# Value tiles of 128 rows at a shift of 15 that serve both the block sums and half of the local attention

## The chip, the cores and the metric

The kernel runs on one core of a Trainium2 chip. The metric is the device time of one execution in microseconds (us), from launch to the last result in memory. Times of a kernel are given as the median of several runs; one further execution is recorded by the hardware profiler, and its rows are what the text quotes. KB and MB in the profile's list of transfers are 1024 and 1024 x 1024 bytes; GB/s are in powers of ten.

## The reference

Attention and a mixture of experts in sequence. Attention: batch 4, 8 heads, 768 positions, head size 64, all in float32. Every query sees the keys less than 16 positions away and, beside them, one summary key for each of the 24 blocks of 32 keys.

```python
k_sum = k.reshape(B, H, nb, block, D).max(axis=3)      # block = 32, nb = 24
v_sum = v.reshape(B, H, nb, block, D).mean(axis=3)
scores_l = scale * np.matmul(q, k.transpose(0, 1, 3, 2))
mask_l = np.abs(pos[:, None] - pos[None, :]) < window  # window = 16
scores_s = scale * np.einsum('bhsd,bhnd->bhsn', q, k_sum) + np.log(block)
scores_all = np.concatenate([np.where(mask_l, scores_l, -1e9), scores_s], axis=-1)
a = softmax(scores_all)
out = np.matmul(a, np.concatenate([v, v_sum], axis=2))
```

The 3072 output rows of 512 go to a noisy top-2 gate with 8 experts, each relu(x @ w1) @ w2 with an inner size of 1024, and the weighted results of the two experts are added.

## The kernel before

**Stages.** Attention takes about the first 145 us of the span, the experts the rest. Attention works on 24 tiles of 128 queries, six tiles to a batch; a tile consists of two blocks of 64 queries (blk 0 and 1). A block of queries needs the 94 keys and values that lie up to 15 positions around it, and the 24 block sums of its batch. The kernel lays both into one row of 118: the sums first (columns 0 to 23), then the 94 local ones. So every score matrix, every exp and every product with the values has 118 columns or rows.

**One step of the loop** (line 896, step t) does pieces of several tiles. TensorE: scores of tile t+2 (`scores`, L296, 32 matmuls of 64 queries by 118 keys, after `mask_sums`, L286, has written the mask of the next tile), transposes of the probabilities of tile t+1 (`p_trans`, L316), transposes of the result of tile t-1 for the gate (`x_pe`, L360), and the product with the values of tile t (`av`, L329). VectorE takes the row maxima (`smax`, L303) and divides (`norm`, L338 to L344). ScalarE does the exps (`sexp`, L310), copies the transposed probabilities (tile pts, L319), copies the transposed result (xt, L366) and makes its high half (xr, L349). GpSimd copies the keys of a tile into the joint row (kx, L114 and L120) and makes the low half of the result (L352). The gate's work for groups of four tiles is scattered between by hand, with `at(time, function)`, and so are the loads of later batches, the block sums and the first expert's weights.

**The values** are in DRAM with a column of ones behind each head (520 numbers a position) and 15 rows of zeros ahead. They are read twice. `load_vn` (L131) brings a batch into SBUF as six tiles of 128 positions (VN, in the memory that later holds the experts' hidden layer, hth). `v_sums` (L237) multiplies them with the 0/1 matrix ind of 24 columns and gets the block sums (48 matmuls, L241). `v_window` (L260) brings, for each block of 64 queries, a window of 96 positions into rows 24 to 119 of a buffer vw or htl; there are twelve such buffers, six for the batches of even and six for those of odd number. The sums are written to rows 0 to 23 of these buffers: for the first batch by VectorE, ScalarE and GpSimd to all six (L249, L250, L253), for a later batch by ScalarE to the first (L247) and by five DMAs of 24 rows to the other five (`v_rest`, L258).

**The order of the transfers** is that of SP's queue, which issues nearly all of them in program order. In step t that is: the query tile t+4 (`load_q`, L108), whatever `at` puts there (keys, L103; value tiles; copies of the sums; weights), the two windows of tile t+3 (`v_load`, after the av of tile t), and the result of tile t-2 (`x_out`, L355). The query tile that is issued in step t is used in step t+2. A window for tiles 3 to 5 of a batch waits until the av of three tiles before has read its buffer, and what stands behind it on SP waits too.

**At the end of attention** the rows of the first expert are gathered from the result in DRAM (xg <- xd, an indirect DMA of GpSimd), transposed by DMA, and the experts' matmuls begin (L727, L773).

Of the kernel before, what the change touches and what calls it, by code (L numbers as in the profile page):

```python
# [8 lines left out]
F32 = mybir.dt.float32  # L9
# [4 lines left out]
AF = mybir.ActivationFunctionType  # L14
# [3 lines left out]
B, H, S, D = 4, 8, 768, 64  # L18
BLK, WIN = 32, 16
NB = S // BLK  # L20
P = 128
TS = S // P
# [7 lines left out]
W = 64 + 2 * (WIN - 1)  # L30
NK = W + NB
PAD = WIN - 1
KW = S + 2 * PAD + 2
VR = 96
VP = S + VR - 64
H0 = 384
# [25 lines left out]
def attn_moe(ctx, tc, qt, kt, vt, wgn, noise, w1, w2, out):  # L62
# [31 lines left out]
    KB, VW, KX = [], [], []  # L94
# [15 lines left out]
    def kx_local(t):  # L110
        b, j = divmod(t, TS)
        k = KB[b % 2][:, :, j * P:j * P + 64 + W]
        for blk in range(2):
            (nc.vector if t < 2 else nc.gpsimd).tensor_copy(KX[t % QN][:, :, blk, NB:NK],  # L114
                                                            k[:, :, 64 * blk:64 * blk + W])

    def kx_sum(t):
        b, j = divmod(t, TS)
        if j < QN:
            (nc.gpsimd if b else nc.vector).tensor_copy(KX[t % QN][:, :, :, 0:NB],  # L120
                                                        KM[b][:, :, None, :].to_broadcast([P, HP, 2, NB]))
# [6 lines left out]
    VN = [flat[0][:, H * (D + 1) * j:H * (D + 1) * (j + 1)] for j in range(TS)]  # L128

    def load_vn(b, j):  # L130
        nc.sync.dma_start(VN[j].rearrange("p (h d) -> p h d", h=H), vt[b, PAD + j * P:PAD + (j + 1) * P])  # L131

# [30 lines left out]
    nc.vector.memset(masks[2][:, W - PAD:W], -1e9)  # L163

    ind = spare[0][:, :TS * NB].rearrange("p (t n) -> p t n", t=TS)
    nc.gpsimd.iota(ind, pattern=[[-P, TS], [BLK, NB]], base=0, channel_multiplier=-1,
# [3 lines left out]
    nc.vector.scalar_tensor_tensor(ind, ind, 0.0, ind0, op0=OP.is_le, op1=OP.mult)  # L170
    iota8 = const.tile([P, E], F32, name="iota8")
# [31 lines left out]
    for i in range(2):  # L203
        VW += [keep.tile([P, H, D + 1], F32, name=f"vw{4 * i + j}") for j in range(4)]
        VW += [flat[1][:, H * (D + 1) * j:H * (D + 1) * (j + 1)].rearrange("p (h d) -> p h d", h=H)
               for j in range(2 * i, 2 * i + 2)]
# [30 lines left out]
    def v_sums(b):  # L237
        pt = psum.tile([P, HP, P], F32, name="pt", bufs=2).rearrange("p a b -> p (a b)")
        for j in range(TS):
            for g in range(4):  # L240
                nc.tensor.matmul(pt[32 * g:32 * g + NB, 0:C4], ind[:, j, :], VN[j][:, C4 * g:C4 * g + C4],  # L241
                                 start=(j == 0), stop=(j == TS - 1), skip_group_check=True)
        x = [y[0:NB].rearrange("p h d -> p (h d)") for y in VW[(b % 2) * 6:(b % 2) * 6 + 6]]
        for g in range(4):
            i, o = pt[32 * g:32 * g + NB, 0:C4], slice(C4 * g, C4 * g + C4)
            if b:
                nc.scalar.activation(x[0][:, o], i, AF.Copy)  # L247
            else:
                nc.vector.tensor_copy(x[0][:, o], i)  # L249
                nc.scalar.activation(x[1][:, o], i, AF.Copy)  # L250
        if b == 0:
            for i in range(2, 6):
                nc.gpsimd.tensor_copy(x[i], x[i % 2])  # L253

    def v_rest(b):
        x = [y[0:NB] for y in VW[(b % 2) * 6:(b % 2) * 6 + 6]]
        for y in x[1:]:
            nc.sync.dma_start(y, x[0])  # L258

    def v_window(blk):  # L260
        b, j = divmod(blk, 2 * TS)
        x = VW[(b % 2) * 6 + j % 6]
        nc.sync.dma_start(x[NB:NB + VR], vt[b, 64 * j:64 * j + VR])
        return x
# [3 lines left out]
    def v_load(t):  # L268
        VX[t] = [v_window(2 * t), v_window(2 * t + 1)]
# [9 lines left out]
    def mask_sums(t):  # L279
        j = t % TS  # L280
        s = SC[t] = gate_space()[:, :, :SK].rearrange("p a (h k) -> p a h k", h=HP)
        for blk in range(2):
            for a in range(2):
                r = slice(64 * a, 64 * a + 64)
                m = masks[1 if (j, blk) == (0, 0) else 2 if (j, blk) == (TS - 1, 1) else 0]
                nc.tensor.matmul(s[64 * blk:64 * blk + 64, a, :, NB:], identb[r, r],  # L286
                                 m[r, None, :].to_broadcast([64, HP, W]), start=True, stop=False,
                                 skip_group_check=True)
# [509 lines left out]
    def at(t, f, *a):  # L798
        todo.setdefault(round(t, 3), []).append((f, a))
# [12 lines left out]
    for j in range(TS):  # L812
        load_vn(0, j)
# [11 lines left out]
    at(-0.9, v_sums, 0)  # L825

# [12 lines left out]
    for b in range(B - 1):  # L839
        for j in range(TS):  # L840
            at((6 * b + KP[j] if b else KP0[j]) + 0.1, k_piece, b + 1, j)
            if j % 3 == 0:
                at(6 * b + KL[j] if b else -1 + j // 3, load_k, b + 1, j, 3)
            at(VL[b][j], load_vn, b + 1, j)
        at(VS[b] + 0.2, v_sums, b + 1)
        at(VS[b] + 1.02, v_rest, b + 1)
# [298 lines left out]
def layout(q, k, v, moe_w_gate, moe_w_noise, moe_noise, moe_w1, moe_w2):  # L1145
# [9 lines left out]
    vp[:, PAD:PAD + S] = v1.transpose(0, 2, 1, 3)  # L1155
    wgn = np.zeros((P, DC, 4 * E), moe_w_gate.dtype)
# [23 lines left out]
```

## Time and profile before

| what | value |
|---|---|
| time, median of 3 runs | 698.92 us (696.99 to 701.62) |
| the profiled execution: its own time, its span | 698.5 us, 696.6 us |
| busy share of the span: PE, DVE, ACT, POOL | 94%, 46%, 34%, 36% |
| moved by DMA over the span | 125.88 MB, mean 181 GB/s |
| loads of value windows (32 to vw, 16 to htl) | 48 of 195 KB |
| loads of value tiles for the sums | 24 of 260 KB |

PE is TensorE, DVE VectorE, ACT ScalarE, POOL GpSimd, SP the engine that issues DMAs; SPq is its queue. An instruction is named by its line in the program, its engine, its operation, and what it writes and reads (out <- in), without buffer numbers. A bracket at the end of a row gives the time for which the engine stood idle ahead of it and what ended that. The chain of work that ended last is followed back from the last instruction to whatever released each step. PE's busy time is modelled, so a high share alone does not say that it is the bound; which wait ends last does.

### The profile page before, as it was taken

How to read it: one execution, taken by the hardware profiler on the slowest of the kernel's cores; microseconds unless marked ns; L12 is line 12 of the kernel's file. 1: busy time of each engine (PE TensorE's matmuls, PEld its weight loads, DVE VectorE, ACT ScalarE, POOL GpSimd, SP SyncE). 2: the span in 40 equal slices, each digit the busy share in tenths (PEclk: the TensorE clock that was granted, in tenths of full speed). 3: DMA queues.
4: the chain of work that ended last, by engine and by line, in shares of the span. 5: the costliest groups of instructions: out<-in, count | busy, mean ns of one | idle time of the engine just before them, and what ended most of it. 6: DMA issues, size and time to landing. Idle time of an engine off the chain costs nothing.

```text
span 696.6 us, 13835 instructions
## 1 busy us (share of the span) xinstructions
PE 654.1 (94%) x5408; PEld 378.9 (54%) x5408; DVE 317.1 (46%) x677; ACT 237.6 (34%) x543; POOL 253.9 (36%) x430
## 2 busy tenths in 40 slices
PE   7798999659899989999999999999999999999995
PEld 6676777535354644465446544654565456446542
DVE  5646788977863254226413521452154125312211
ACT  2887899744022143015202410340044015102200
POOL 3344366340531531553144323424350433222031
PEclk9999999989999999999999999999999999999999
DMA  9999897679555792559525951793199239421021
GB/s 278 316 256 319 273 317 230 200 141 403 139 174 117 187 320 77 171 181 283 189 94 132 219 191 71 176 253 133 63 247 220 94 109 272 109 79 60 1 88 47
DMA packets 101991, 125.88 MB, mean 181 GB/s; under 512 B 58621, under 2 KB 63493, under 8 KB 101916
## 3 DMA queue, kind: packets, MB, share of 16 engines
q1 hardware_dynamic: 90236, 88.64, 46.7%
q0 software_dynamic: 11680, 36.27, 17.4%
q8 instruction: 44, 0.72, 0.4%
q14 instruction: 31, 0.25, 0.1%
HBM read 86.82 MB, written 25.82 MB: 162 GB/s over the span
## 4 chain that ended last, share of the span: by engine, by line
PE 71%; issue 8%; DMA 7%; DVE 5%; POOL 4%; ACT 4%; SPq 1%; POOLq 0%; DVEq 0%; ACTq 0%
PE h L727 32%; PE pt L773 32%; DMA q<-in_qt_dram 3%; ACT p L310 2%; PE pt L769 2%; PE s L296 2%; DMA xg<-xd,tb 2%; PE o L329 1%; POOL kx L114 1%; POOL out_dram L87 1%; DMA kb<-in_kt_dram 1%; PE pt L316 1%; DVE w2l L665 1%; ACT pts L319 1%; DMA htl<-in_vt_dram 1%
## 5 line engine op out<-in xcount | busy, mean ns | idle before, releaser
L727 PE MATMUL h<-xte,w1h 128*128 128x384 f16 (+4 forms) x1024 | 197.3, 334 | 6.7 <-DMA xte<-xg 4.7
L731 ACT ACTIVATE hth<-h 128x384 f16<-128x384 f32 (+4 forms) x128 | 63.6, 500 | 317.5 <-PE h L727 309.7
L87 POOL DMA_INDIRECT out_dram<-y,tb x48 | 56.1, 1168 | 261.4 <-DVE y L782 231.4
L727 PEld LDWEIGHTS <-w1h 128*128 128x128 f16 x1024 | 100.3, 99 | 80.0 <-issue 10.0
L773 PEld LDWEIGHTS <-hth 128*128 128x128 f16 x768 | 75.1, 98 | 93.1 <-issue 3.9
L732 DVE SCALAR_TENSOR_TENSOR htl<-h,hth 128x384 f16<-128x384 f32 (+4 forms) x128 | 72.3, 569 | 102.4 <-ACT hth L731 91.2
L727 PE MATMUL h<-xte,w1l 128*128 128x384 f16 (+4 forms) x512 | 108.2, 334 | 0.0
L782 DVE SCALAR_TENSOR_TENSOR y<-pt,tb,prev 128x512 f32<-128x512 f32 x42 | 31.5, 751 | 168.0 <-PE pt L773 168.0
L773 PE MATMUL pt<-w2l,hth 128*128 128x512 f16 x384 | 91.2, 379 | 2.8 <-DVE w2l L665 2.8
L773 PE MATMUL pt<-w2h,hth 128*128 128x512 f16 x384 | 90.7, 379 | 0.0
L773 PE MATMUL pt<-w2h,htl 128*128 128x512 f16 x384 | 90.7, 379 | 0.0
L87 POOL DMA_INDIRECT xg<-xd,tb x53 | 59.5, 1123 | 70.5 <-DMA xte<-xg 41.6
L727 PEld LDWEIGHTS <-w1l 128*128 128x128 f16 x512 | 50.5, 99 | 36.7 <-issue 1.4
L773 PEld LDWEIGHTS <-htl 128*128 128x128 f16 x384 | 37.6, 98 | 45.0
L352 POOL TENSOR_TENSOR xr<-x,xr 128x512 f16<-128x512 f32 x24 | 28.2, 1174 | 69.4 <-ACT xr L349 61.2
L310 ACT ACTIVATE p<-s,nm 128x118 f32<-128x118 f32 x192 | 50.7, 376 | 0.8
L648 ACT ACTIVATE w2h<-stg 128x1024 f16<-128x1024 f32 x32 | 33.6, 1053 | 50.5 <-DMA stg<-in_w_dram 50.5
L665 DVE SCALAR_TENSOR_TENSOR w2l<-stg,w2h 128x1024 f16<-128x1024 f32 x32 | 38.8, 1221 | 23.2 <-ACT w2h L648 21.3
L87 POOL DMA_INDIRECT prev<-out_dram,tb x42 | 43.9, 1046 | 13.2 <-issue 13.2
L665 DVE SCALAR_TENSOR_TENSOR w1l<-stg,w1h 128x1024 f16<-128x1024 f32 x28 | 34.3, 1225 | 14.4 <-ACT w1h L648 13.6
L296 PE MATMUL s<-kx,q 64*64 64x118 f32 x768 | 28.4, 280 | 9.7 <-DMA q<-in_qt_dram 5.2
L316 PE MATMUL pt<-ident,p 128*118 128x128 f32 x192 | 29.3, 289 | 4.5 <-DVE lg L394 1.9
(173 smaller groups left out, 557.8 us busy)
## 6 DMA issues: line engine op xcount, KB each, us to landing
stg<-in_w_dram SPq DMA_DIRECT2D x64, 512.0 KB
hth<-in_vt_dram SPq DMA_DIRECT2D x24, 260.0 KB
vw<-in_vt_dram SPq DMA_DIRECT2D x32, 195.0 KB
q<-in_qt_dram SPq DMA_DIRECT2D x24, 256.0 KB
xd<-xr SPq DMA_DIRECT2D x24, 256.0 KB
out_dram<-xg SPq DMA_DIRECT2D x8, 768.0 KB
kb<-in_kt_dram SPq DMA_DIRECT2D x6, 768.0 KB
htl<-in_vt_dram SPq DMA_DIRECT2D x16, 195.0 KB
```

The source lines that it names most:

```text
L87: return nc.gpsimd.indirect_dma_start(**kw)
L296: nc.tensor.matmul(s[64 * blk:64 * blk + 64, a, hp, :], q[d, hp, blk], k[d, hp, blk, :], start=False, stop=hp == HP - 1, skip_group_check= ...
L310: nc.scalar.activation(PE_[t][:, a, hp, :], SC[t][:, a, hp, :], AF.Exp, bias=NM[t][:, 1, a, hp:hp + 1], scale=0.125)
L316: nc.tensor.transpose(pt[:NK, hp, :], PE_[t][:, a, hp, :], ident)
L352: nc.gpsimd.tensor_tensor(XR[t][:, DM:], X[t], XR[t][:, 0:DM], op=OP.subtract)
L648: nc.scalar.activation(WT[e][n + "h"][:, i % 4, :], SG[e, i], AF.Copy, scale=sc)
L665: nc.vector.scalar_tensor_tensor(lo, SG[e, i], sc, hi, op0=OP.mult, op1=OP.subtract)
L727: nc.tensor.matmul(ph[:, :n], w[wn][:, c, f * P:(f + 1) * P], x[:, xo + c, c0:c1], start=(k == 0), stop=(k == 11))
L731: nc.scalar.activation(hh[:, f, c0:c1], ph[:, :n], AF.Relu)
L732: nc.vector.scalar_tensor_tensor(hl[:, f, c0:c1], ph[:, :n], 0.0, hh[:, f, c0:c1], op0=OP.max, op1=OP.subtract)
L773: nc.tensor.matmul(py, hx[:, f, c * P:c * P + P], wv[:, f, :], start=(k == 0), stop=(k == 23))
L782: nc.vector.scalar_tensor_tensor(y, py[:, :d], gw, pv[:, :d], op0=OP.mult, op1=OP.add)
```

## The change

**One tile for two purposes.** The value tiles of 128 rows now begin 15 positions earlier: row r of tile j is position 128 j - 15 + r. Rows 0 to 95 are then the window of the tile's first block of 64 queries. The same tile serves the block sums, and once these are summed, they are written over its rows 96 to 119. So the first block's row of 120 is 96 local values and then 24 sums, and its keys are laid out in this order too (`L0[0] = 0`). The second block keeps a window of its own (VD), sums first, local values behind (`L0[1] = 24`). Both use 96 local keys instead of 94, with a mask that is two columns wider; NK goes from 118 to 120.

**The shift in the sums.** The six tiles of a batch cover positions -15 to 752. The last 15 positions are put in DRAM into the 15 rows ahead of the first, which were zeros; ind starts 15 later, and one column of it is set to 1 in rows 0 to 14 of the first tile. In the local attention of the batch's first block those rows are masked, as the zeros were.

**Buffers and transfers.** The value tiles have two buffers (VE, one in the memory of hth, one of its own), since they now live until the av of their tile. The windows are three for each parity of the batch (VD), one for a tile. The first batch's sums are copied by GpSimd to tiles 1 and 2 and to all windows, and by a DMA to tiles 3 to 5 (`v_rest(0)`, new in step 0). For a later batch one DMA writes five tiles and three write the windows. A tile's `v_load` issues one window.

```diff
-W = 64 + 2 * (WIN - 1)
+W = 64 + 2 * WIN
-    KB, VW, KX = [], [], []
+    KB, KX = [], []
+    L0 = (0, NB)
...
-            (nc.vector if t < 2 else nc.gpsimd).tensor_copy(KX[t % QN][:, :, blk, NB:NK],
+            (nc.vector if t < 2 else nc.gpsimd).tensor_copy(KX[t % QN][:, :, blk, L0[blk]:L0[blk] + W],
...
-    VN = [flat[0][:, H * (D + 1) * j:H * (D + 1) * (j + 1)] for j in range(TS)]
-
-    def load_vn(b, j):
-        nc.sync.dma_start(VN[j].rearrange("p (h d) -> p h d", h=H), vt[b, PAD + j * P:PAD + (j + 1) * P])
+    VE = [flat[0][:, :TS * VB].rearrange("p (j c) -> p j c", j=TS), keep.tile([P, TS, VB], F32, name="ve")]
+    VD = [[flat[1][:, VB * j:VB * (j + 1)] for j in range(3)],
+          [keep.tile([P, VB], F32, name=f"vd{j}") for j in range(2)] + [flat[1][:, 3 * VB:4 * VB]]]
+
+    def load_ve(b, j):
+        nc.sync.dma_start(VE[b % 2][:, j].rearrange("p (h d) -> p h d", h=H), vt[b, j * P:(j + 1) * P])
...
+    nc.vector.memset(ind[0:PAD, 0, NB - 1:NB], 1.0)
...
-        x = [y[0:NB].rearrange("p h d -> p (h d)") for y in VW[(b % 2) * 6:(b % 2) * 6 + 6]]
+        x, y = VE[b % 2][W:W + NB], [z[0:NB] for z in VD[b % 2]]
...
-                nc.scalar.activation(x[0][:, o], i, AF.Copy)
+                nc.scalar.activation(x[:, 0, o], i, AF.Copy)
             else:
-                nc.vector.tensor_copy(x[0][:, o], i)
-                nc.scalar.activation(x[1][:, o], i, AF.Copy)
+                nc.vector.tensor_copy(x[:, 0, o], i)
+                nc.scalar.activation(y[0][:, o], i, AF.Copy)
         if b == 0:
-            for i in range(2, 6):
-                nc.gpsimd.tensor_copy(x[i], x[i % 2])
+            for i in range(1, 3):
+                nc.gpsimd.tensor_copy(x[:, i], x[:, 0])
+                nc.gpsimd.tensor_copy(y[i], y[0])
 
     def v_rest(b):
-        x = [y[0:NB] for y in VW[(b % 2) * 6:(b % 2) * 6 + 6]]
-        for y in x[1:]:
-            nc.sync.dma_start(y, x[0])
-
-    def v_window(blk):
-        b, j = divmod(blk, 2 * TS)
-        x = VW[(b % 2) * 6 + j % 6]
-        nc.sync.dma_start(x[NB:NB + VR], vt[b, 64 * j:64 * j + VR])
-        return x
+        x = VE[b % 2][W:W + NB]
+        j = 1 if b else 3
+        nc.sync.dma_start(x[:, j:], x[:, 0, None, :].to_broadcast([NB, TS - j, VB]))
+        if b:
+            for y in VD[b % 2]:
+                nc.sync.dma_start(y[0:NB], x[:, 0])
...
     def v_load(t):
-        VX[t] = [v_window(2 * t), v_window(2 * t + 1)]
+        b, j = divmod(t, TS)
+        y = VD[b % 2][j % 3].rearrange("p (h d) -> p h d", h=H)
+        nc.sync.dma_start(y[NB:NB + VR], vt[b, P * j + 64:P * j + 64 + VR])
+        VX[t] = [VE[b % 2][:, j].rearrange("p (h d) -> p h d", h=H), y]
...
     at(-0.9, v_sums, 0)
+    at(0.8, v_rest, 0)
...
+    vp[:, :PAD] = vp[:, S:S + PAD]
```

**Where rows move on SP.** Names with a number are buffers; rows are in the order of issue, and x3 stands for three in a row. First, SP in steps 0 and 1, up to the query tile of tile 5 (q_93, the last row). The kernel before:

```order
L131 DMA hth<-in_vt_dram 128x520 x3
L103 DMA kb_89<-in_kt_dram 128x4x384
L103 DMA kb_88<-in_kt_dram 128x4x384
L263 DMA vw_158<-in_vt_dram 96x520
L263 DMA vw_159<-in_vt_dram 96x520
L108 DMA q_93<-in_qt_dram 128x512
```

The changed kernel at the same place:

```order
L136 DMA ve<-in_vt_dram 128x520 x3
L105 DMA kb_89<-in_kt_dram 128x4x384
L105 DMA kb_88<-in_kt_dram 128x4x384
L261 DMA hth<-hth 24x3x520
L271 DMA htl<-in_vt_dram 96x520
L110 DMA q_93<-in_qt_dram 128x512
```

One window of tile 3 is gone ahead of the query tile, and the copy of the first batch's sums to three tiles has come in. Earlier in the queue, in the opening, six windows have become three.

Second, SP in steps 4 and 5, where the second batch's sums are copied (from the query tile of tile 8 to that of tile 9). The kernel before:

```order
L108 DMA q_96<-in_qt_dram 128x512
L258 DMA vw_163<-vw_162 24x520
L258 DMA vw_164<-vw_162 24x520
L258 DMA vw_165<-vw_162 24x520
L258 DMA htl<-vw_162 24x520 x2
L131 DMA hth<-in_vt_dram 128x520 x2
L263 DMA vw_164<-in_vt_dram 96x520
L263 DMA vw_165<-in_vt_dram 96x520
L355 DMA xd<-xr 128x1024
L108 DMA q_97<-in_qt_dram 128x512
```

The changed kernel:

```order
L110 DMA q_96<-in_qt_dram 128x512
L261 DMA ve<-ve 24x5x520
L264 DMA vd_99<-ve 24x520
L264 DMA vd_100<-ve 24x520
L264 DMA htl<-ve 24x520
L136 DMA hth<-in_vt_dram 128x520 x2
L271 DMA vd_100<-in_vt_dram 96x520
L358 DMA xd<-xr 128x1024
L110 DMA q_97<-in_qt_dram 128x512
```

Five copies of 24 rows have become four, which write eight places; two windows have become one. Third, SP in steps 6 and 7, up to the query tile of tile 11 (q_94). The kernel before:

```order
L131 DMA hth<-in_vt_dram 128x520
L103 DMA kb_89<-in_kt_dram 128x4x384
L263 DMA vw_162<-in_vt_dram 96x520
L263 DMA vw_163<-in_vt_dram 96x520
L355 DMA xd<-xr 128x1024
L108 DMA q_94<-in_qt_dram 128x512
```

The changed kernel:

```order
L136 DMA hth<-in_vt_dram 128x520
L105 DMA kb_89<-in_kt_dram 128x4x384
L271 DMA vd_99<-in_vt_dram 96x520
L358 DMA xd<-xr 128x1024
L110 DMA q_94<-in_qt_dram 128x512
```

Again one window less stands ahead of the query tile; the rest of the order is as before.

More of the change, by code (lines that the diff above doesn't have):

```diff
@@ L29 @@
 HP = H // 2
-W = 64 + 2 * (WIN - 1)
+W = 64 + 2 * WIN
 NK = W + NB
 PAD = WIN - 1
-KW = S + 2 * PAD + 2
+KW = S + 2 * WIN
 VR = 96
 VP = S + VR - 64
+VB = H * (D + 1)
 H0 = 384
@@ L119, in kx_sum @@
         if j < QN:
-            (nc.gpsimd if b else nc.vector).tensor_copy(KX[t % QN][:, :, :, 0:NB],
+            x = KX[t % QN].rearrange("p h b k -> p h (b k)")[:, :, W:W + 2 * NB]
+            (nc.gpsimd if b else nc.vector).tensor_copy(x.rearrange("p h (b n) -> p h b n", b=2),
                                                         KM[b][:, :, None, :].to_broadcast([P, HP, 2, NB]))
@@ L162, in attn_moe @@
     nc.vector.memset(masks[1][:, 0:PAD], -1e9)
-    nc.vector.memset(masks[2][:, W - PAD:W], -1e9)
+    nc.vector.memset(masks[2][:, 64 + PAD:], -1e9)
     ind = spare[0][:, :TS * NB].rearrange("p (t n) -> p t n", t=TS)
-    nc.gpsimd.iota(ind, pattern=[[-P, TS], [BLK, NB]], base=0, channel_multiplier=-1,
+    nc.gpsimd.iota(ind, pattern=[[-P, TS], [BLK, NB]], base=PAD, channel_multiplier=-1,
                    allow_small_or_imprecise_dtypes=True)
@@ L202, in attn_moe @@
         nc.gpsimd.memset(x[:, :, PAD + S:], 0.0)
[L203 to L206, printed above, removed]
     late = []
@@ L240, in v_sums @@
             for g in range(4):
-                nc.tensor.matmul(pt[32 * g:32 * g + NB, 0:C4], ind[:, j, :], VN[j][:, C4 * g:C4 * g + C4],
+                nc.tensor.matmul(pt[32 * g:32 * g + NB, 0:C4], ind[:, j, :], VE[b % 2][:, j, C4 * g:C4 * g + C4],
                                  start=(j == 0), stop=(j == TS - 1), skip_group_check=True)
-        x = [y[0:NB].rearrange("p h d -> p (h d)") for y in VW[(b % 2) * 6:(b % 2) * 6 + 6]]
+        x, y = VE[b % 2][W:W + NB], [z[0:NB] for z in VD[b % 2]]
         for g in range(4):
@@ L285, in mask_sums @@
                 m = masks[1 if (j, blk) == (0, 0) else 2 if (j, blk) == (TS - 1, 1) else 0]
-                nc.tensor.matmul(s[64 * blk:64 * blk + 64, a, :, NB:], identb[r, r],
+                nc.tensor.matmul(s[64 * blk:64 * blk + 64, a, :, L0[blk]:L0[blk] + W], identb[r, r],
                                  m[r, None, :].to_broadcast([64, HP, W]), start=True, stop=False,
@@ L812, in attn_moe @@
     for j in range(TS):
-        load_vn(0, j)
+        load_ve(0, j)
     for u in range(3):
@@ L843, in attn_moe @@
                 at(6 * b + KL[j] if b else -1 + j // 3, load_k, b + 1, j, 3)
-            at(VL[b][j], load_vn, b + 1, j)
+            at(VL[b][j], load_ve, b + 1, j)
         at(VS[b] + 0.2, v_sums, b + 1)
```

## The prediction

> **What bounds the kernel now.** I first read how busy the engines and the DMA engines are along the span, in a table by stages (columns: stretch in us, its length, busy us and instructions of PE (TensorE), PEld (its weight loads), DVE (VectorE), ACT (ScalarE) and POOL (GpSimd), granted clock of TensorE, share of the 16 DMA engines in use, GB/s).
>
> ```profile
> 25.00:45.00 20.00, 17.89 (x335) 14.00 (x332) 12.75 (x24) 15.64 (x49) 6.64 (x12) 0.91 1.04 301
> 45.00:68.00 23.00, 19.58 (x393) 15.27 (x391) 14.45 (x45) 20.81 (x67) 11.36 (x18) 1.00 0.95 293
> 68.00:110.00 42.00, 39.12 (x818) 31.25 (x820) 34.11 (x109) 36.12 (x115) 22.27 (x31) 1.00 0.95 290
> 110.00:145.00 35.00, 27.14 (x510) 20.86 (x508) 31.92 (x95) 28.84 (x87) 19.65 (x26) 1.00 0.62 191
> 190.00:690.00 500.00, 497.42 (x2788) 262.00 (x2786) 176.66 (x255) 113.87 (x176) 169.97 (x286) 1.00 0.57 152
> ```
>
> From 190 us on, TensorE works 497.4 of 500 us on the experts, which the change does not touch. So only the attention stage, up to about 145 us, can give or take time, and what it gives passes to the end undiminished, because the expert stage has no slack to soak it up. In attention the DMA engines are full up to 110 us (share 0.95 to 1.04, 290 to 301 GB/s from 25 us on) while TensorE and ScalarE are nearly full too. Only a wait can tell which of them ends last. The chain of work that ended last (start, duration, what) has three transfers in that stage that stand out, and TensorE's timeline places two of them.
>
> ```profile
> 1.98 6.42 DMA kb<-in_kt_dram
> ...
> 26.43 8.88 DMA q<-in_qt_dram
> ...
> 59.45 8.64 DMA q<-in_qt_dram
> ```
>
> ```profile
> 32.28 1.16 PE L329 MATMUL o<-htl,pts 118*64 118x65 f32 x32
> 35.45 1.37 PE L296 MATMUL s<-kx,q 64*64 64x118 f32 x32 [2.01 <-DMA q<-in_qt_dram]
> 36.75 1.96 PE L316 MATMUL pt<-ident,p 128*118 128x128 f32 x8
> ...
> 63.91 1.15 PE L329 MATMUL o<-htl,pts 118*64 118x65 f32 x32
> 68.22 1.04 PE L296 MATMUL s<-kx,q 64*64 64x118 f32 x32 [3.16 <-DMA q<-in_qt_dram]
> 69.19 1.09 PE L316 MATMUL pt<-ident,p 128*118 128x128 f32 x8
> ```
>
> The first is the opening load of the keys, ahead of everything that changes. The other two are query tiles that come late: that of tile 5 (issued 26.43, landed 35.31) and that of tile 11 (issued 59.45, landed 68.09). In brackets stands TensorE's idle time before the scores, 2.01 and 3.16 us. TensorE had finished the work ahead at 32.28 + 1.16 = 33.44 and 63.91 + 1.15 = 65.06. Each load needed almost 9 us for 256 KB, which at 300 GB/s is 0.9 us. The rest is the line of transfers ahead of it on SP's queue. A second price hangs on the first wait: the eight transposes behind it took 1.96 us against 1.09 behind the second.
>
> **The change part by part: bytes.** It takes away one of two 96-row value windows for each of the 24 tiles, and it copies the sum rows into more places.
>
> ```profile
> hth<-in_vt_dram SPq DMA_DIRECT2D x24, 260.0 KB
> vw<-in_vt_dram SPq DMA_DIRECT2D x32, 195.0 KB
> q<-in_qt_dram SPq DMA_DIRECT2D x24, 256.0 KB
> ...
> htl<-in_vt_dram SPq DMA_DIRECT2D x16, 195.0 KB
> ...
> vw<-vw SPq DMA_DIRECT2D x9, 48.8 KB
> htl<-vw SPq DMA_DIRECT2D x6, 48.8 KB
> ```
>
> Removed: 24 x 195 = 4680 KB. The copies of the 24 sum rows go from 15 blocks of 48.8 KB to 3 + 3 x (5 + 3) = 27, so 12 blocks or 585 KB are added. What counts is what stands ahead of the two late loads.
>
> Ahead of tile 5's load, three windows of the opening and one of tile 3 go (780 KB), and the first batch's copy of three blocks comes in (146 KB). Net 634 KB = 649 kB, at 301 GB/s 2.2 us. The load was 35.31 - 33.44 = 1.9 us late: the wait should just go, with 0.3 us to spare. Ahead of tile 11's load, six further windows go (1170 KB) and the second batch's copies grow from five blocks to eight (146 KB): net 1024 KB = 1049 kB, at 293 GB/s 3.6 us. The load would land at 68.09 - 2.2 - 3.6 = 62.3.
>
> **What the waits are worth.** ScalarE is the fuller engine here, and it catches up during each wait, so I follow its rows.
>
> ```profile
> 32.25 2.11 ACT L310 ACTIVATE p<-s,nm 128x118 f32<-128x118 f32 x8
> 34.20 0.65 ACT L366 ACTIVATE xt<-pt 128x512 f32<-128x512 f32 x1
> 34.68 0.69 ACT L349 ACTIVATE xr<-x 128x512 f16<-128x512 f32 x1
> ...
> 38.75 0.60 ACT L319 ACTIVATE pts<-pt 118x512 f32<-118x512 f32 x1 [0.26 <-PE pt L316]
> ...
> 65.76 0.65 ACT L366 ACTIVATE xt<-pt 128x512 f32<-128x512 f32 x1
> 67.43 0.63 ACT L349 ACTIVATE xr<-x 128x512 f16<-128x512 f32 x1 [1.02 <-DMA xd<-xr]
> 67.97 0.19 ACT L445 ACTIVATE p<-d 128x4 f32<-128x4 f32 x1
> 69.88 1.09 ACT L319 ACTIVATE pts<-pt 118x512 f32<-118x512 f32 x2 [1.73 <-PE pt L316]
> ```
>
> First wait: the pair of pts copies ended at 38.75 + 0.60 = 39.35. Without the wait ScalarE is free at 34.68 + 0.69 = 35.37 and needs 1.08 us for them: 36.45. Gain 2.9 us, the slow transposes included. Second wait: it ended at 69.88 + 1.09 = 70.97. Without it, xr would start 0.48 us after xt, as at 34.20 and 34.68, and end at 66.9, L445 at 67.1 and pts at 68.2: gain 2.8. That needs the xd write, on which xr waited until 67.43, to be earlier too. It lies in the same full queue, so it should be. After the first gain TensorE wants tile 11's load at 65.06 - 2.9 = 62.2 and the bytes give 62.3. But not all bytes saved are time saved: in the stretch with the old copies the engines stood partly idle.
>
> ```profile
> 40.00:50.00 10.00, 9.82 (x220) 7.71 (x212) 5.40 (x10) 9.45 (x31) 3.73 (x6) 1.00 0.85 248
> ```
>
> Idle share 0.15 of 10 us is 1.5 us that fewer bytes cannot shorten. So the remaining wait is 0.1 to 1.6 us; I charge 0.6, nearer the low end since SP also issues 26 fewer transfers in all (24 windows, and 13 copies for 15).
>
> **Rows that grow.** Local keys go from 94 to 96 and a score row from 118 to 120. Beside the exps and scores above, VectorE's maximum over 8 x 118 columns grows; its group of rows (count, busy us, mean ns, idle before):
>
> ```profile
> L303 DVE TENSOR_REDUCE nm<-s 128x8 f32<-128x944 f32 x24 | 27.2, 1135 | 7.2 <-PE s L296 7.2
> ```
>
> If time went with columns, a tile would cost 2.11 x 2/118 = 0.036 us more on ScalarE, 0.019 on VectorE (1135 x 16/944) and 0.018 on TensorE (1.04 x 2/118). All in one chain for 24 tiles is 1.8 us; if fixed cost rules the instructions, nothing. I take ScalarE's alone over the some 20 tiles where it is the fullest engine: 0.7 us. At nothing I cost the memset of one column of ind (it stands ahead of VectorE's wait for the keys, which land at 1.98 + 6.42 = 8.4 us), the transposes (the 128 columns of ident still move through), the av matmuls (65 columns as before), and the sums written at rows 96 to 119, which keep their 24 x 130 shapes and their number. The value loads get a second buffer, but the old one was free in time, so this alone gives nothing.
>
> **The sum.** The profiled execution took 698.5 us around a span of 696.6, and it lies 0.4 under the median of 698.92. 698.5 - 2.9 - 2.8 + 0.6 + 0.7 = **694.1 us**.
>
> **Where a copy of 24 rows is dear.** SP's own rows bound the price of such a block from above.
>
> ```profile
> 43.03 2.52 SPq L258 DMA_DIRECT2D vw<-vw  x3
> 46.71 1.76 SPq L258 DMA_DIRECT2D htl<-vw  x2
> ```
>
> Five blocks held SP from 43.03 to 48.47, 1.1 us each; at the full rate a block is 0.17 us. I take the low end, since those rows include waits for earlier transfers. [...]
>
> **The rivals.** First, *another wait takes the place* (chance 0.2). Right behind tile 5's load stand the next batch's value tiles, three of 260 KB (799 kB, 2.7 us), which the block sums read once the scores (1.04) and the transposes (1.09) are through: from 33.44 that is 35.6. With tile 5's load at 33.1 they land at 35.8, just about when TensorE asks for them. If these, or tile 11's load, are late by 1.5 us each, half of the gain is gone: 694.1 + 2.4 = 696.5. For it: the queue stays nearly full. Against it: in the kernel as it is no such wait shows.
>
> Second, *slower: the copies* (0.12). If a block of sum rows costs SP's queue 1.1 us, tile 5's load gets 3 x 1.1 = 3.3 us more against 4 x 0.7 = 2.8 less, and lands later than now; at 0.93 us a block the two are even. Tile 11's load stays about as late as now, and the wider rows cost their upper bound: 698.5 + 0.5 + 1.8 = 700.8.
>
> Third, *more than the waits* (0.12). At the end of attention an indirect gather is on the chain.
>
> ```profile
> 143.76 7.30 DMA xg<-xd,tb
> ```
>
> If the window loads are what fills the DMA engines there too, and the gather took half, 3.6 us would be added: 694.1 - 3.6 = 690.5. Against it: the DMA share is only 0.62 from 110 to 145 us, where the last windows are loaded.
>
> Fourth, *the transfers were hidden anyway* (0.06): the query loads are late by their fixed order behind a tile's av and not by bytes, and nothing but the wider rows is left: 698.5 + 0.7 = 699.2.
>
> **How the numbers follow.** My forecast has 0.5, its own range 692 to 697. To leave out no more than 2 in 10 the range must take in the first and fourth rivals and the edge of the third: 690.5 to 699.5. One per cent of the median (7 us), about what a measurement of this kernel can tell from no change, lies outside nearly all of these: the third rival with a little more reaches it (faster 0.13), the second only with new waits in later batches (slower 0.06), and the rest is within (0.81).
>
> **What would show it.** Right: no wait of TensorE on a query load over 1 us; the transposes of tile 4 at 1.1 us; the attention stage 4 to 5 us shorter at its end; the eight exps of a tile at 2.11 to 2.15 us; DMA share clearly below 0.95 between 68 and 110 us; the stretch behind attention shifted but no shorter. Wrong: a wait on the value tiles of the block sums, on the copies of the sums, or a query load that still takes 8 us; or a first transposed gather that gains more than attention did.

## The result, and the profile after

The changed kernel took 693.13 us (median of 7 runs, 690.3 to 694.24) beside 698.78 us of the kernel before (7 runs, 695.55 to 701.62): a ratio of 0.992, 95% interval 0.9893 to 0.9948. A second time it was 692.03 (6 runs, 690.62 to 693.2) beside 698.52 (0.9883, 0.9847 to 0.9919). The forecast was 694.1. (Ratios and intervals are given as they were recorded; they are not the quotients of the medians, from which they differ by up to 0.0024.) The profiled execution took 694.24 us around a span of 692.4, against 698.5 and 696.6 before.

First the table by stages, in the same columns as before.

```profile
25.00:45.00 20.00, 19.49 (x401) 15.29 (x401) 13.86 (x25) 18.24 (x59) 8.39 (x15) 1.00 0.95 277
45.00:68.00 23.00, 21.80 (x452) 17.29 (x450) 17.11 (x54) 21.88 (x70) 13.52 (x20) 1.00 0.89 285
68.00:110.00 42.00, 39.11 (x778) 30.61 (x780) 35.77 (x103) 37.75 (x117) 23.21 (x30) 1.00 0.83 250
110.00:145.00 35.00, 27.16 (x480) 21.53 (x480) 30.33 (x107) 25.14 (x73) 17.82 (x26) 0.90 0.49 150
190.00:690.00 500.00, 492.98 (x2767) 259.91 (x2765) 172.00 (x243) 113.40 (x176) 171.43 (x287) 0.99 0.57 151
```

The DMA engines are now the less full side: 0.83 in use from 68 to 110 us (0.95 before) and 0.49 from 110 to 145 (0.62). TensorE and ScalarE did more in the same 23 us from 45 to 68 (21.80 and 21.88 us busy, 19.58 and 20.81 before), since they no longer stand. TensorE's timeline at the two places of the prediction, the scores of tiles 5 and 11:

```profile
34.00 1.05 PE L299 MATMUL s<-kx,q 64*64 64x120 f32 x32
34.98 1.23 PE L319 MATMUL pt<-ident,p 128*120 128x128 f32 x8
36.14 0.36 PE L289 MATMUL s<-mask,identb 64*64 64x384 bf16 x4
36.56 1.53 PE L243 MATMUL pt<-ve,hth 128*24 128x130 f32 x48
...
62.26 1.05 PE L299 MATMUL s<-kx,q 64*64 64x120 f32 x32
63.24 1.14 PE L319 MATMUL pt<-ident,p 128*120 128x128 f32 x8
```

Neither score row has a bracket for a query load. The transposes behind the first take 1.23 us (1.96 before), and the block sums of the second batch (L243), which the first rival expected to wait for their value tiles, run straight through. ScalarE's rows at the same places:

```profile
32.90 2.12 ACT L313 ACTIVATE p<-s,nm 128x120 f32<-128x120 f32 x8
34.86 0.65 ACT L369 ACTIVATE xt<-pt 128x512 f32<-128x512 f32 x1
35.34 0.69 ACT L352 ACTIVATE xr<-x 128x512 f16<-128x512 f32 x1
35.86 1.14 ACT L322 ACTIVATE pts<-pt 120x512 f32<-120x512 f32 x2
...
63.03 0.65 ACT L369 ACTIVATE xt<-pt 128x512 f32<-128x512 f32 x1
63.51 0.69 ACT L352 ACTIVATE xr<-x 128x512 f16<-128x512 f32 x1
64.03 0.26 ACT L448 ACTIVATE p<-d 128x4 f32<-128x4 f32 x1
64.13 1.14 ACT L322 ACTIVATE pts<-pt 120x512 f32<-120x512 f32 x2
```

It goes from one row to the next as the forecast had it, with xr 0.48 us behind xt at both places.

The query tile of tile 5 is not issued earlier than before (27.56 us, before 26.43): SP is held at the keys' load until GpSimd has read older keys, for 5.1 us in the change and 2.1 before. What shrank is the time from issue to landing: 8.88 us before, and in the change at most 6.4, since the scores begin at 34.00. The query tile of tile 11 is issued earlier (54.95 us, before 59.45). For that load the chain of before has one more row, which does not stand with the prediction: its issue follows at once on the landing of a value window.

```profile
53.97 5.47 DMA htl<-in_vt_dram
```

The chain that ended last has lost both query tiles. Of the transfers up to 200 us two are left in it (start, duration, what), the opening load and a result that is written when the experts begin.

```profile
1.99 6.18 DMA kb<-in_kt_dram
...
152.46 7.98 DMA out_dram<-xg
```

The gather of the third rival is not among them. In the second profile of the change it is, and took 6.46 us (7.30 before):

```profile
138.66 6.46 DMA xg<-xd,tb
```

I split the attention stage by the starts of the scores (tile 2, 4, ...) and the first matmul of the experts; each length is the difference of two starts in TensorE's timeline, in us. The rows from the third on are runs told below.

| kernel | 2 to 4 | 4 to 6 | 6 to 12 | 12 to 17 | 17 to 20 | 20 to 23 | 23 to experts |
|---|---|---|---|---|---|---|---|
| before | 10.1 | 13.2 | 33.5 | 23.8 | 16.6 | 19.4 | 20.1 |
| changed | 10.7 | 9.9 | 30.7 | 23.8 | 16.8 | 21.3 | 18.8 |
| changed, second profile | 10.4 | 9.9 | 30.6 | 23.8 | 16.8 | 19.9 | 19.2 |
| all windows again | 10.1 | 13.3 | 33.9 | 23.8 | 16.8 | 19.4 | 18.3 |
| windows 0 to 3 again | 10.8 | 15.8 | 30.7 | 23.8 | 16.8 | 19.4 | 20.2 |
| windows 4 to 9 again | 12.9 | 9.7 | 32.6 | 23.8 | 16.8 | 19.4 | 18.9 |
| windows 10 to 23 again | 10.7 | 9.9 | 30.6 | 23.8 | 16.8 | 19.3 | 19.0 |
| before, rows of 120 | 10.2 | 14.5 | 37.0 | 23.8 | 16.6 | 19.3 | 18.6 |

The gain is 3.3 us between tiles 4 and 6 and 2.8 us between tiles 6 and 12, where the two waits were; 0.5 us are lost ahead of them. From tile 12 to 20 another 0.3 us go, and from tile 20 on variants with the same program differ among themselves by as much as the change and the kernel before. The 12.9 us from tile 2 to 4 with windows 4 to 9 is hardly the work of these windows: in that profile TensorE's clock was at half from 23.3 to 30.1 us, and the first of the windows was issued at 28.79.

### The profile page after: what moved, and what is told of

It is laid out like the page before. It is cut to its first block, busy times and chain, and to the rows that moved or that the text cites. A ratio compares the mean times of both kernels' runs of the same rounds, so it can differ in the third digit from the quotient of the medians.

```text
span 692.4 us, 13782 instructions
## 1 busy us (share of the span) xinstructions
PE 655.3 (95%) x5408; PEld 379.8 (55%) x5408; DVE 318.1 (46%) x678; ACT 237.3 (34%) x543; POOL 255.1 (37%) x430
## 4 chain that ended last, share of the span: by engine, by line
PE 71%; DVE 7%; issue 7%; ACT 5%; POOL 4%; DMA 4%; SPq 1%; POOLq 0%; DVEq 0%
PE h L730 32%; PE pt L776 32%; ACT p L313 2%; PE s L299 2%; PE pt L772 2%; DMA stg<-in_w_dram 1%; PE o L332 1%; ACT pts L322 1%; DMA out_dram<-xg 1%; POOL kx L116 1%; DVE w2l L668 1%; POOL out_dram L88 1%; DMA kb<-in_kt_dram 1%; PE pt L319 1%; PE pt L363 1%
## 5 line engine op out<-in xcount | busy, mean ns | idle before, releaser
L313 ACT ACTIVATE p<-s,nm 128x120 f32<-128x120 f32 x192 | 51.0, 377 | 0.8
L88 POOL DMA_INDIRECT prev<-out_dram,tb x42 | 45.3, 1080 | 13.3 <-issue 13.3
L299 PE MATMUL s<-kx,q 64*64 64x120 f32 x768 | 29.7, 285 | 5.2 <-DVE kx L123 3.2
L319 PE MATMUL pt<-ident,p 128*120 128x128 f32 x192 | 28.6, 283 | 4.6 <-DVE lg L397 1.9
```

The lines of the kernel that those rows point to most:

```text
L88: return nc.gpsimd.indirect_dma_start(**kw)
L299: nc.tensor.matmul(s[64 * blk:64 * blk + 64, a, hp, :], q[d, hp, blk], k[d, hp, blk, :], start=False, stop=hp == HP - 1, skip_group_check= ...
L313: nc.scalar.activation(PE_[t][:, a, hp, :], SC[t][:, a, hp, :], AF.Exp, bias=NM[t][:, 1, a, hp:hp + 1], scale=0.125)
L319: nc.tensor.transpose(pt[:NK, hp, :], PE_[t][:, a, hp, :], ident)
```

## The experiments

The theory to be tested is that of the prediction: the two query tiles were late by the bytes ahead of them in a full queue. Its rival is the place in the queue: they were late because they are issued behind a tile's av and its windows, and some other part of the change freed them. Ratios below are to the kernel before, run on the same chip.

**The windows loaded again: all, and in three parts.** The changed kernel keeps its layout, and for the named tiles t the lost transfer of 96 rows is issued at its old place, into rows that hold the same data or a buffer that is filled later, so that nothing of the result changes.

```diff
     def v_load(t):
         b, j = divmod(t, TS)
         y = VD[b % 2][j % 3].rearrange("p (h d) -> p h d", h=H)
+        if t >= 0:                          # t < 4, 4 <= t < 10, t >= 10 in the other three
+            z = VE[b % 2 if t > 2 else 1][:, j].rearrange("p (h d) -> p h d", h=H)
+            nc.sync.dma_start(z[0:VR], vt[b, P * j:P * j + VR])
```

> The changed kernel, with the 24 windows of 96 rows that the change took away loaded once more at their old places in the queue (into rows that hold or receive the same data; 24 x 195 KB come back, the result is the same). Layout, rows of 120 columns and copies of the sums stay as changed. Theory of bytes: TensorE waits again on the query tiles of tiles 5 and 11, 1.5 to 3.5 us each, and the time is 697 to 700 us, about that of the kernel before plus the wider rows. Rival, the loads were late by their place behind a tile's av and another part of the change freed them: no wait on a query tile over 1 us, 693 to 694 us.

> The changed kernel with the windows of tiles 0 to 3 alone loaded once more (780 KB, all ahead of the query tile of tile 5). Theory of bytes: that load lands 2.2 to 2.7 us later, the wait on it comes back with 1 to 2.5 us, none on the query tile of tile 11 (TensorE asks for it later by as much), and 2.0 to 3.5 us are lost: 695 to 696.6 us. Rival (place, not bytes): 693 to 693.6 us.

> The changed kernel with the windows of tiles 4 to 9 alone loaded once more (1170 KB, all behind the query tile of tile 5 and ahead of that of tile 11). Theory of bytes: no wait on tile 5's query tile, one of 1.5 to 3.5 us on tile 11's, 2.0 to 3.3 us lost: 695 to 696.5 us. Rival (place, not bytes): 693 to 693.6 us.

> The changed kernel with the windows of tiles 10 to 23 alone loaded once more (2730 KB, behind the query tile of tile 11). Theory of bytes ahead of two late loads: no wait comes back and the time is that of the changed kernel within 0.7 us, 692.5 to 694 us, although more than half of the saved bytes are moved again. Rival (every byte saved gives time, in the gather at the end of attention too): 2 to 4 us lost, 695 to 697 us.

| windows again for tiles | median of 12 runs, us | ratio, interval |
|---|---|---|
| all | 700.02 | 1.0011 (0.9977 to 1.0045) |
| 0 to 3 | 697.14 | 0.9958 (0.9927 to 0.9989) |
| 4 to 9 | 695.8 | 0.9971 (0.9942 to 0.9999) |
| 10 to 23 | 692.89 | 0.9923 (0.9894 to 0.9951) |
| none (the change, first time, 7 runs) | 693.13 | 0.992 (0.9893 to 0.9948) |
| none (second time, 6 runs) | 692.03 | 0.9883 (0.9847 to 0.9919) |

With all windows the kernel is back at the time of before, and TensorE's timeline shows both waits again, the first at 35.45 us, as before:

```profile
35.45 1.05 PE L302 MATMUL s<-kx,q 64*64 64x120 f32 x32 [2.02 <-DMA q<-in_qt_dram]
36.43 1.64 PE L322 MATMUL pt<-ident,p 128*120 128x128 f32 x8
...
68.50 1.05 PE L302 MATMUL s<-kx,q 64*64 64x120 f32 x32 [2.19 <-DMA q<-in_qt_dram]
```

With tiles 0 to 3 alone only the first wait is there, and with tiles 4 to 9 alone only the second. Their rows in TensorE's timeline are, of the first:

```profile
38.16 1.72 PE L302 MATMUL s<-kx,q 64*64 64x120 f32 x32 [3.86 <-DMA q<-in_qt_dram]
```

and of the second:

```profile
65.75 1.05 PE L302 MATMUL s<-kx,q 64*64 64x120 f32 x32 [2.08 <-DMA q<-in_qt_dram]
```

The last variant moves 14 of the 24 windows again (2730 KB, more than half of what the change saves), shows no wait on a query tile and has the time of the change. So by the medians the bytes ahead of tile 5's load are worth 4.2 us (697.14 against 692.89) and those ahead of tile 11's 2.9 us (695.8 against 692.89); by the ratios it is 2.4 and 3.4 us. Which of the two is worth more is therefore not shown, but each is worth some microseconds, and all other bytes are worth nothing that these runs can tell. With tiles 0 to 3 the median lies above the 695 to 696.6 that I expected and the wait of 3.86 us above the 1 to 2.5; a run further below shows that this wait varies by itself. The added transfers also have a wait of their own: with tiles 4 to 9, SP is held at one of them for 0.9 us until the block sums have read their tile, so not all of that loss need be bytes. The rival of the place falls for the change: the order of the issues was the same in all these rows but for the added windows.

**The query tiles one step earlier, on the kernel before.** The same bytes, another order.

```diff
-QA = 4
+QA = 5
```

> The kernel before with every query tile issued one step earlier (five buffers for four), the same bytes and all else as before. If the place in the queue alone made the two query loads late, both waits go and the time falls as with the change, to 692.5 to 694 us. Theory of bytes: the queue is full, so the two waits on query tiles go but what now stands behind them (windows, value tiles for the sums, keys) is late in their place: 695.5 to 699 us.

695.69 us (median of 12; ratio 0.9951, 0.9921 to 0.998). By the ratio some 3.4 us are won, where the change won 5.6. No query tile is waited for, but what now stands behind them is late. TensorE waits for the value tiles of the second batch's sums:

```profile
37.08 0.42 PE L241 MATMUL pt<-hth 128*24 128x130 f32 x8 [0.67 <-DMA hth<-in_vt_dram]
38.24 0.42 PE L241 MATMUL pt<-hth 128*24 128x130 f32 x8 [0.74 <-DMA hth<-in_vt_dram]
```

and ScalarE, at the second place, for the write of a result that frees the buffer of xr:

```profile
68.26 0.63 ACT L349 ACTIVATE xr<-x 128x512 f16<-128x512 f32 x1 [2.65 <-DMA xd<-xr]
```

In the kernel before that wait was 1.02 us. From tile 6 to tile 12 this variant takes 34.9 us, more than before (33.5): there the wait changed its place, and TensorE's clock was at half from 69.9 to 73.3 us behind it. So the place in the queue counts too: the order alone wins part of the time, and part of the lateness moves to what now stands behind. This is the mechanism of my first rival, on a kernel without the change.

**Copies of the sum rows twice.**

```diff
     def v_rest(b):
+        rest(b)
+        rest(b)
+
+    def rest(b):
```

> The changed kernel with each copy of the sum rows by DMA issued twice (27 more blocks of 24 rows, 48.8 KB each, the result is the same). At 0.17 us a block (its bytes at the full rate, as the forecast has it) three blocks more ahead of tile 5's query tile cost 0.5 us and eight more ahead of tile 11's 1.4 us, which mostly find room: 693 to 694.5 us. At 1.1 us a block, the slow rival's price, the waits on both query tiles come back with over 2 us each: 697 us or more.

703.04 us (12 runs; 1.0042, 1.0013 to 1.0072): 3.0 us above the kernel before on the same chip, so all that the change won is lost, and more. But this run costs something that I had not meant. The second copy writes where the first does, so SP holds it until the first has landed, and all that stands behind on SP waits too, as SP's row for the first batch's pair shows:

```profile
26.12 6.87 SPq L265 DMA_DIRECT2D hth<-hth  x2
```

So it does not price a block by the total. It does so elsewhere: the second set of eight blocks, issued from 50.14 us on, ran alone in a queue that had emptied (DMA share 0.09 from 49 to 51 us). The table by windows for 2.2 us of it:

```profile
51.60:53.80 2.20, 2.20 (x66) 1.97 (x61) 1.18 (x4) 1.61 (x5) 1.22 (x3) 1.00 0.70 135
```

Here the blocks of 24 rows moved at 135 GB/s (DMA share 0.70), under half of the 277 to 301 GB/s of the stages up to 68 us. At that rate eight blocks (390 KB, 399 kB) are 3.0 us, 0.37 us a block. My forecast had 0.17, the slow rival 1.1. What sets the price is not shown: SP issued these transfers from 50.14 to 53.63 us, about as long as the eight blocks took, so the issue may have set it. And the wait behind such copies lands on the next query tile, that of tile 9, in TensorE's timeline:

```profile
60.97 1.88 PE L303 MATMUL s<-kx,q 64*64 64x120 f32 x32 [4.06 <-DMA q<-in_qt_dram]
```

**Rows of 120 alone, on the kernel before.**

```diff
-W = 64 + 2 * (WIN - 1)
+W = 64 + 2 * WIN
```

(and the mask of a batch's last block made wider by the same two columns).

> The kernel before with 96 local keys for 94, so rows of 120 columns for 118, and nothing else of the change; the loads stay as they were. The forecast's term: 0.7 us slower, 1.8 at most, so a ratio of 1.001 (to 1.0026). Theory from the two traces (starts of the scores of tiles 11 and 19 to 21 shift by 0.3 us against each other): 0.0 to 0.3 us, a ratio of 1.0000 to 1.0005. The waits on the query tiles of tiles 5 and 11 stay, and take up what the rows grow ahead of them.

700.32 us (12 runs; 1.0017, 0.9984 to 1.005): the interval holds both 0.2 and 0.7 us, so the time does not decide. The sections say more, where no load is waited for. From tile 12 to 17 the kernel before takes 23.77 us, this one 23.81, the change 23.82: 0.01 us a tile. The profile shows something else as well. Its loads are those of the kernel before, and the waits of TensorE on query tiles are 7.9 us in three places, where the profile of before has 5.2 in two:

```profile
PE s L296 <- DMA q<-in_qt_dram: 7.9, 3, 4.0
```

**The copies on GpSimd at the opening.** In the change the scores of tile 3 start 6.23 us behind those of tile 2 (25.34 and 19.11), before 5.73 (24.73 and 19.00). TensorE's timeline names the keys, which GpSimd copies behind the sums:

```profile
25.34 1.49 PE L299 MATMUL s<-kx,q 64*64 64x120 f32 x32 [0.96 <-POOL kx L116]
```

So I moved the last two of the four copies behind these keys, and ran it twice, the second time beside the changed kernel.

```diff
-            for i in range(1, 3):
-                nc.gpsimd.tensor_copy(x[:, i], x[:, 0])
-                nc.gpsimd.tensor_copy(y[i], y[0])
+            sums_to(1)
...
+    at(0.1, sums_to, 2)
```

> The changed kernel with the first batch's copies of the sums to the third value tile and the third window moved on GpSimd behind the keys of tile 3. Theory: the 0.6 us by which the scores of tile 3 start later than in the kernel before come from these copies ahead of the keys on GpSimd, so the scores of tile 3 start at 24.3 to 24.8 us and the time falls by 0.5 to 1.0: 692.1 to 692.6 us. Rival (the 0.6 us come from the loads ahead): no change, 693.1 us.

> The changed kernel with the first batch's sums for tile 2 copied behind the keys of tile 3, once more, now on one chip with the changed kernel. Theory: the earlier 691.3 us were a gain of 0.5 to 1.5 us, since the scores of tile 3 no longer wait for GpSimd: it is again below the changed kernel by that. Rival: in its profile the keys of tile 3 still come in pieces and the scores take 1.8 us for 1.5, so nothing was gained and the two are within 0.4 us.

> The changed kernel itself once more, on the same chip as the three others, as their measure. If the stretch at half clock between 127 and 135 us belongs to the change it stands there again with the same length (two units of 3.4 us). If it is chance, its place or length differs, as it does in the profiles of the other variants, whose program is the same there. Time: 692.5 to 694 us beside 698.5 to 700 of the kernel before.

691.3 and 691.29 us (6 runs each; 0.9886, 0.9851 to 0.992, and 0.9888, 0.9847 to 0.9929), and the changed kernel beside the second 692.03 (6 runs; 0.9883). 691.3 lies below the 692.1 to 692.6 expected, but so does the change itself, beside the second, below the 692.5 to 694 expected of it. Beside each other the two are 0.7 us apart by the medians and 0.0005 by the ratios, so no gain is shown. In the first of the profiles the bracket is gone, but the row is longer (1.82 us, with the change 1.49; whether by keys that still come in pieces or by the half clock named below is not shown):

```profile
23.78 1.82 PE L302 MATMUL s<-kx,q 64*64 64x120 f32 x32
```

and from tile 2 to 4 it takes 10.8 us, as the change does (10.7 and 10.4). TensorE's clock was at half from 22.0 to 25.4 us in that profile, so even this is not a clean comparison. The rows place the 0.5 us of the opening: the four copies start 3.09 us behind tile 2's scores (before 2.93) and take 2.64 us (before 2.30), so in the change they end 5.73 us behind tile 2's scores, before 5.23. With two of them moved the scores of tile 3 start 6.0 and 5.5 us behind those of tile 2, yet nothing is won by tile 4. So that the delay of tile 3 costs the kernel anything is not shown.

**The query tiles earlier, with the change.** The kernel just told, with `QA = 5` as well.

> As the run before, and every query tile issued one step earlier (five buffers for four), which on the kernel before moved the wait from the query tiles to the value tiles of the sums (1.4 us) and to the write of the results (2.65 us). Theory of bytes: with 4.7 MB fewer in the queue there is room for that, neither wait shows, and the query wait that still stands in some executions of the change goes as well: 690 to 691.5 us, equal to or up to 1 us below the run before. Rival: the waits take the other places here too, 692 to 694 us.

694.25 us (8 runs; 0.9928, 0.9894 to 0.9962), with the changed kernel at 692.03 and the kernel just told at 691.29 on the same chip. The rival had it better, though its 692 to 694 is missed too, and of its two places only the first shows: ScalarE does not wait for the write of a result. TensorE's waits between 28 and 70 us (in all, times, longest) name no query tile any more, but value tiles:

```profile
PE pt L243 <- DMA ve<-in_vt_dram: 1.2, 2, 0.8
```

The queue is not so empty by then that its order could be changed for nothing. No variant of these runs is shown to be faster than the change.

**Filling TensorE's gaps.** In the profile of the change the clock is at half between 127.3 and 134.1 us, and the section from tile 20 to 23 is 1.9 us longer than before. I added small matmuls on a constant that were to fill the gaps ahead.

```diff
+    BUSY = {19: (18, 12, 0), 20: (8, 0, 16)}
...
+            if t in BUSY:
+                busy(t - 1, BUSY[t][0])
```

> The changed kernel with some 60 small matmuls on a constant between the pieces of tiles 18 to 20, where TensorE has gaps (their result is overwritten). Theory: in the profile of the change the granted clock falls to half between 127 and 135 us after such gaps and this costs 1.9 us; with the gaps filled the clock stays at 1.00 there and the time falls by 1 to 2 us: 691 to 692 us. Rival (the fall of the clock is chance and not tied to the gaps, or what it costs is regained before the experts begin): 693 us or more, as the matmuls themselves cost time.

694.46 us (8 runs; 0.9918, 0.9886 to 0.995), no better than the change. The clock still fell, from 128.2 to 131.6 us in its profile. But this run does not test the theory. The first 18 of the matmuls write into a tile that VectorE is still to read, and TensorE stood idle ahead of them:

```profile
127.13 0.68 PE L362 MATMUL o<-identb 128*128 128x64 bf16 x18 [3.66 <-DVE acc L557]
```

At that place of the program the change has a gap of 1.45 us. So the gap was made longer and not filled, and 1.05 us of TensorE's work are left in the 3.41 us ahead of the fall. The time lies in the rival's range, but whether filled gaps would keep the clock stays open. This profile taught something else: up to tile 18 its program is that of the change, and yet TensorE waits for the query tile of tile 5.

```profile
37.08 1.88 PE L299 MATMUL s<-kx,q 64*64 64x120 f32 x32 [3.64 <-DMA q<-in_qt_dram]
```

The second profile with late copies on GpSimd has a shorter wait at the same place:

```profile
34.55 1.05 PE L302 MATMUL s<-kx,q 64*64 64x120 f32 x32 [1.61 <-DMA q<-in_qt_dram]
```

Neither of these loads was issued late: at 26.38 and 25.01 us, where the change issued its at 27.56.

## Why the prediction was right, point by point

- **The bound, and that no slack swallows the gain: right.** The experts' first matmul starts at 151.09 us instead of 155.70, and the span ends 4.2 us earlier. The windows of tiles 0 to 3 and of tiles 4 to 9, brought back, each cost a part of the gain, and all windows together the whole; those of tiles 10 to 23 cost nothing.
- **First wait, 2.9 us: right.** Against the start of tile 4's scores (0.63 us later than before) the pair of pts copies ends at 37.00 instead of 39.35, which is 3.0 us earlier. By the start of tile 6 it is 3.3, since the half clock behind the old wait (granted clock 0.50 from 36.0 to 39.4 us) slowed a little more than the transposes: the mask of the next tile took 0.53 us there and 0.36 in the change.
- **Second wait, 2.8 us: right.** The pair ends at 65.27 instead of 70.97, of which 2.84 were won at tile 10 already: 2.86 us. That xr's wait on the xd write goes too was a condition of that step. It holds with fewer bytes (no bracket on xr at 63.51), and fails when only the order is changed (2.65 us).
- **A remaining wait of 0.6 us at tile 11: wrong place.** Six profiles have the windows of tiles 0 to 9 gone and the order of the change, and in none of them does TensorE wait for tile 11's query tile. But seven profiles have the change's transfers up to tile 5 (the change twice, the late copies on GpSimd twice, the filled gaps, windows 4 to 9 and 10 to 23 again), and two of these wait at tile 5: 3.64 us in the one above, 1.61 us in the second with late copies. I had given that load 0.3 us to spare and called its wait gone. It is gone in five of these seven profiles; over all seven it is (3.64 + 1.61) / 7 = 0.75 us a profile. That this comes near the 0.6 charged for the other tile is luck.
- **Wider rows, 0.7 us: too much.** Eight exps take 2.12 us where they took 2.11, not the 2.15 of time by columns. VectorE's maximum did grow as its columns do (L306 took 1152 ns, before 1135). Yet a tile grows by 0.01 us only from 12 to 17. The term was meant for ScalarE, whose rows hardly grew, and the lower end of that step was nearer.
- **What was costed at nothing: the copies at the opening.** That the copies of the sums keep their number overlooked that those of GpSimd end 0.5 us later, ahead of the keys for which TensorE waits, and tile 4 starts 0.5 us later behind tile 2. What of it reaches the end is not shown, as no gain shows with two of the copies moved.
- **The price of a block of sum rows: 0.37 us, not 0.17.** Three blocks more ahead of tile 5's load are then 1.1 us and not 0.5, more than the 0.3 to spare. That fits a wait there in some executions, but no run separates it from the queue's own variation.
- **The rivals.** *More than the waits* fell: with the last 14 windows moved again, the stretch from tile 23 to the experts is 19.0 us, with the change 18.8 and 19.2: no loss from those bytes shows at the gather. *Hidden anyway* fell with the four variants, *slower* with the result and with the price of a block. *Another wait takes the place* did not happen to the change, but did to both variants that changed the order.
- **The sum.** Profile against profile 4.3 us were won and 4.4 forecast. That they agree so closely is luck: errors of 0.3 to 0.6 us of both signs cancelled, among them 0.6 us lost from tile 20 on, where the forecast had nothing and profiles of the same program differ. The medians differ by 5.7 and 6.5 us, so the forecast gain was too small by 1.3 and 2.1. One profile of before is one draw of its waits: the profile with the same loads and rows of 120 shows 2.7 us more of them. That before loses more by its waits in the median than in the one profile that I read is likely, but it is argued from these two profiles, and from the spread of the times beside each other: 695.06 to 705.13 us in 19 runs of before, 690.62 to 693.2 in 6 of the change.

What stays open: why the query tile of tile 5 is late in two executions of seven with the same transfers ahead of it.

## What to carry to other kernels

In a queue that is full, look for the few loads that an engine waits for, and count the bytes ahead of each: in these runs bytes taken away ahead of them were time, and bytes taken away behind them were not (692.89 us with the last 14 windows loaded again, 693.13 and 692.03 without). A new order alone moved the wait to what then stood behind; it won a part of the time where the queue was full (ratio 0.9951), and nothing once the bytes were gone (694.25 us, 691.29 without it). Give such a load more room than its lateness in one profile, since the wait on it varied by microseconds from execution to execution (at tile 5 none, 1.61 and 3.64 us with the same transfers ahead). Work that is to fill a gap needs a place of its own to write to: here it wrote into a tile that VectorE was still to read, and TensorE stood idle for 3.66 us ahead of it. And before a difference between two profiles is explained, compare the sections of variants that run the same program there.

## What the runs showed of the hardware: half clock on a grid of 3.41 us

The stretches at half clock in the attention stage begin and end on a grid. In each of the 14 profiles of this case those that can be placed to 0.1 us lie whole multiples of 3.41 us apart, and the grid's phase differs from execution to execution: 36.02, 152.06 and 158.9 us before; 127.32, 134.14 and 147.80 after. What sets the clock at a border of the grid no run shows; what can be told is how much work TensorE had in the 3.41 us ahead of each stretch. The table by windows cut on this grid, for the first wait of the kernel before (PE busy is the first sum, the clock the third number from the end):

```profile
29.20:32.61 3.41, 3.34 (x60) 2.44 (x60) 3.25 (x7) 3.38 (x11) 1.38 (x2) 1.00 1.08 275
32.61:36.02 3.41, 1.40 (x52) 1.29 (x51) 1.70 (x5) 2.76 (x10) 1.24 (x3) 1.00 1.07 289
36.02:39.43 3.41, 3.41 (x40) 2.41 (x35) 2.33 (x3) 1.28 (x3) 1.76 (x4) 0.50 1.06 237
```

and for the second:

```profile
63.33:66.74 3.41, 1.74 (x41) 1.43 (x39) 1.93 (x6) 3.04 (x11) 1.27 (x3) 1.00 1.07 325
66.74:70.15 3.41, 1.93 (x40) 1.69 (x40) 0.83 (x1) 0.99 (x3) 2.01 (x3) 1.00 0.87 286
70.15:73.56 3.41, 2.79 (x86) 2.25 (x84) 2.91 (x13) 3.37 (x13) 1.22 (x4) 1.00 1.01 313
```

The first wait, of 2.01 us, lay inside one window, which was left with 1.40 us of work, and the next window ran at half clock: the slow transposes of the prediction. The second wait was longer (3.16 us), but a border at 66.74 us cut it in two, both windows kept 1.74 us of work or more, and the clock stayed at 1.00. Over all windows between 20 and 165 us at full clock in the 14 profiles, each cut in this way on its own grid, all 28 with less than 1.65 us of modelled TensorE work were followed by one at half clock, and none of the 468 with more than 1.89 us; between the two, four of ten were. These are counts of this case, no rule.

This bears on the stretch that I tried to fill, too. In the profile of the change and in that with the last windows again (same program from tile 20 on) it stands at different places. With the change:

```profile
123.91:127.32 3.41, 1.88 (x28) 1.06 (x19) 3.27 (x18) 3.41 (x10) 1.11 (x2) 1.00 0.68 205
127.32:130.73 3.41, 2.81 (x40) 2.49 (x42) 2.17 (x4) 2.04 (x9) 0.94 (x3) 0.50 0.22 85
130.73:134.14 3.41, 3.41 (x49) 2.72 (x45) 1.54 (x7) 2.21 (x7) 1.41 (x5) 0.50 0.49 138
```

and with the last windows again:

```profile
117.17:120.58 3.41, 0.94 (x8) 0.53 (x8) 3.34 (x7) 1.43 (x4) 2.63 (x3) 1.00 0.96 305
120.58:123.99 3.41, 3.37 (x44) 2.95 (x48) 3.34 (x20) 2.15 (x9) 0.00 (x0) 0.50 0.18 61
```

In the first it lasts two windows and tile 20 to 23 takes 21.3 us; in the second one window, beside work of VectorE that fills it anyway (3.34 of 3.41 us busy), and the section takes 19.3 us, as before. The second profile of the change has it for two windows again, but from 119.4 to 126.2 us, and takes 19.9 us from tile 20 to 23. So what the stretch costs goes with its place on the grid, and differs for one and the same program; that the place is the cause is argued from these profiles. Whether the stretch as such belongs to the change is not settled: no profile of the kernel before, of its two variants, with all windows or with doubled copies has one that begins between the scores of tile 20 and those of tile 23, and all others have.
